# Expert attention with queries on partitions, masked scores in SBUF and 32x64 PE tiles, in a two-stage attention kernel

## The chip, the cores and the metric

One core of a Trainium2 chip runs the whole program. The metric is the time of one execution on the device, in microseconds (us), as the median over runs; for the kernel before it is 646.24 us. "PE" is TensorE's matmul stream, "PEld" its weight loads, DVE is VectorE, ACT is ScalarE, POOL is GpSimd, SP is the SyncE queue that issues nearly all DMAs.

## What is computed

Two attentions in sequence. The first has 4 batches, 8 heads, 768 positions and 64 dimensions; a query only sees keys that fall into its own one of 16 clusters. Its output is `x`, 4 x 768 x 512. The second has 4 experts with causal attention over `x`, each with its own projections, and a gate that keeps two experts a position:

```python
# stage 1, for each batch and head
q_assign = argmax(q_n @ c_n.T); k_assign = argmax(k_n @ c_n.T)
scores = where(q_assign[:, None] == k_assign[None, :], q @ k.T / 8, -1e9)
x_head = softmax(scores) @ v
# stage 2, for each expert e of 4
q, k, v = x @ wq[e], x @ wk[e], x @ wv[e]        # 512 -> 64
scores = where(causal, -1e9, q @ k.T / 8)
ye = softmax(scores) @ v @ wo[e]                  # 64 -> 512
out += (weight of e at this position, 0 if it isn't among the top two) * ye
```

The factors of wq and wk make the second stage's scores large, so its softmax subtracts the true row maximum, and both stages split an operand into a rounded high part and a remainder (`hi`, `lo`) and multiply three products (hi by lo, hi by hi, lo by hi).

## The kernel before

The work is cut into 24 pairs of heads: pairs 0 to 15 are the first stage (four a batch), pairs 16 to 23 the second (two pairs of experts a batch, `ep` 0 and 1). Each step is written as an operation of a `Plan`: its engine, what it needs, which buffers it uses. The order in which operations are issued, over all engines, is a list of numbers written out by hand (`ORDER`; a star picks the other engine that an operation may run on), and a second list (`SLOTS`) says which slot of its tag each buffer gets. Each engine runs its own instructions in that order; PSUM is four slots of two banks (tag `pp`).

Both kinds of pair go through `core(n)` (L829). It has two passes over the scores.

- **The row pass** puts queries on partitions to find each query's maximum: matmuls at L873 (first stage) and L877 (experts: 16 matmuls a pair, of the high parts alone, of 128 to 512 key columns, as the causal triangle needs), for experts the diagonal block's mask added in PSUM (L886), a DVE maximum over the keys (L888), a reduction (L898) and a 32x32-block transpose (L921, L923), and a DMA that writes the maxima as row 48 of the mask half of the tile `tk`.
- **The second pass** puts keys on partitions: for each block of 128 keys the three products and a fourth, `km` by `qm`, that subtracts the maximum and, in the first stage, applies the cluster mask (L960: 8 matmuls a block, of 384, 256 or 128 query columns). ACT takes the exponential from PSUM into a `p` tile (L966), POOL clears the upper triangle of a diagonal block (L971), POOL or DVE adds the `p` tiles of a half up in `acc` (L326, L327: the two engines of one helper), and PE multiplies `p` with the values in fp32 (L1004; `p,vt` in the first stage, `p,vm` for experts), the two heads side by side in two column tiles of 64. An expert pair has nine such blocks: three of the first half (384, 256, 128 columns), six of the second (four of 384, then 256 and 128).

The row sums come from four matmuls of `acc` with ones (L1044, `total`), which stand at the head of the next pair's value product. They go to SBUF (L1048), to DRAM (`sd`) and back as `r`, are inverted (L1067, for experts times the gate `g`), go to DRAM again (`rd`) and come back broadcast over partitions as `rb`; the product with the value result is `xt` in the first stage (L1095), which is stored as `x`. The very last expert pair takes a form of its own without DRAM (`last_half`, L790 to L812). `moe_operands` makes the projections (L666) and `moe_values` the experts' values and gates (L706); `moe_out` multiplies with `wo` (L1133).

Each of the three sets of operands `tk`, `tq` serves every third pair. There are nine `p` tiles, used in turn; one holds 2 x 384 columns.

Of the kernel before, what the change touches and what calls it, by code (L numbers as in the profile page):

```python
# [10 lines left out]
def _warn_once_fixed(msg, *args, **kwargs):  # L11
# [19 lines left out]
MO = dict(pair=25.0, k=-49.5, q=-56.0, v=-45.5, v_step=1.7, x=-43.5, row=-36.5, row_step=2.2, top=30.5, av=17.5,  # L31
          add=40.5, sums=-11.5, norm=52.0, out=26.0, out_step=5.5, keep=10.0, slack=0.05, m_copy=0.1, m_rest=2,
          m_add=4, m_moe=0, m_xt=1, enter=4.0)

ORDER = """
0 19 ~34 1 4 2 31 ~7 5 8 7 56 6 11* 9 3 10 32 12 ~17 20 13* 16* 33 21 55 22 54 35 34 ~13 60 14 147 39 18* 23 61 17* 24
62* 15* ~21 25 148 29 28* 41* 27 30* ~8 70 74 71 68 36 75 80 38 242 72 69 37 78 73 57 79 59 76 58 87 77 63 93 335 85
40 81 94 82 42* 88 83 44 84 86 64 91 241 105 92 100 106 45 114 101 46 108 115 102 109 47 95 103 111 96 104 89 112 117
90 97 66* 98 150 99 243 107 430 48 49 118 121 51 52* 110 53 244 162 50 133 122 163 336 158 134 113 119 159 160 120 127
161 156 116 128 166 43 157 130 167 124 131 123 164 125 136 165 146 168 169 65* 338 170 137 138 561 126 188 145 139 152  # L40
129 177 186 189 140 178 171 187 191 132 172 141 175 200 192 176 142 173 201 135 197 174 179 198 181 144 180 194 190
143 182 195 203 183 154* 184 149 185 151 193 655 196 222 204 213 258 223 537 254 259 219 205 199 255 260 547 220 216
261 560 252 153* 217 214 253 250 215 256 251 225 218 257 228 226 548 275 229 262 231 276 221 245 263 246 232 264 233
224 67 206 234 227 337 294 240 155 271 235 295 202 282 272 236 269 265 283 237 285 230 266 429 280 286 270 288 281
247* 273 289 291 274 267 292 239 207 284 297 268 238 277 278 248* 279 431 432 748 287 308 307 290 298* 367 309 354 368
536 310 538 355 350 311 293 319 208 351 299 352 320 313 353 312 348 314 209 346 349 316 347 344 317 315 322 345 323
325 356 357 318 326 358 327 211 535 300 328 321 550 329 374 334* 296 330 361 388 375 331 362 359 551 389 210 376 360
654 363 324 377 379 364 365 380 369 366 382 340 370 385 332 339 342* 333 301 383 562 386 391 371 372 378 563 373 302
341 437 381 402 401 392* 444 403 384 413 303 445 438 414 416 439 842 541 440 387 417 404 441 448 405 446 449 410 390
447 442 411 407 443 406 408 419 450 451 420 452 305 421 409 393 422 412 423 470 249 428* 461 656 471 482 304 462 459  # L50
483 468 415 394 460 424 479 306 469 425 463 473 480 549 418 464 457 474 453 458 476 434 472 454 455 427 477 485 426
456 475 465 466 395 467 436* 936 478 498 486 495* 579 499 577 580 496 396 481 749 578 594 497 507 595 543 573 508 484
501 574 539 575 502 569 576 397 510 500 570 571 511 504 487 572 433 503 505 513 581 582 514 552 583 515 540* 506 488
516 399 517 599 343 522* 509 518 590 607 600 591 584 608 542* 604 585 519 398 586 605 489 601 587 512 588 602 592 589
613 565 521 593 610 603 490 520 611 596 597 614 616 598 567 545 751 606 564 843 657 435 609 638 617 212 626 673 491
639 665 544* 674 629 612 666 669 1031 630 627 670 671 628 632 672 554 663 631 633 667 664 641 668 635 642 492 684 636
675 644 634 658 645 659 676 646 615 677 493 647 637 685 701 648 698 702 653* 640 680 699 693 681 649 678 695 694 679
650 643 688 618 696 686 689 707 566* 687 682 651 704 619 683 652 705 697 690 845 708 710 691 750 692 660* 620 568 700
721 711 720 759 722 621 661* 723 760 937 761 724 729 762 763 725 730 726 764 757 727 767 1030 758 703 735 768 765 736
732 766 728 752 769 770 753 771 706 733 738 739 740 494 731 712 741 742 709 801 747 743 772 787 802 744 773 734 782  # L60
622 788 774 789 775 795 745 790 737 783 746 792 796 713 776 793 778 755* 777 798 779 780 799 804 781 791 784 785 939
786 623 938 624 714 794 625 815 715 805 814 859 754* 816 817 860 855 818 820 716 856 797 861 821 851 862 829 806 556
558 400 852 853 819 830 826 854 823 827 800 857 824 832 858 863 822 864 833 865 834 803 662 835 825 883 841* 836 874
884 889 875 717 837 872 866 890 828 873 838 881 756 867 892 882 886 893 831 868 887 870 869 839 895 847 885 807 871
876 896 840 898 877 888 878 879 808 844 880 1033 718 809 1032 546* 891 1563 923 908 810 899 947 924 964 948 911 849*
846 965 951 912 909 952 894 945 910 920 946 26 955 921 949 956 913 917 950 953 918 914 954 557* 941 897 915 926 927
957 958 928 959 916 1125 919* 929 989 935 922 962 990 975 930 900 963 966 811 976 980 967 931 812 968 977 981 969 932
925 960 901 978 970 961 986 1564 971 983 848* 933 934 902 984 972 973 987 992 974 1565 940 979 1124 943* 1005 993 1002
# [3 lines left out]
1028 1062 1056 524 1063 1075 1086 905 1027 1035 1057 942* 1066 1067 1068 1076* 906 1037* 1087 1154 1139 1096 1155 1088  # L72
1102 526 1140 1133 1079 1103 1097 1132 1134 1135 1098 1099 1136 559* 1143 1100 1082 1111 1144 998 1141 1112 1158 1142
1108 523 1101 1159 1137 1109 1105 1138 1085 1106 1114 1145 1146 1115 1147 1104 1116 1117 1107 1118 1174 1123 944 1127
553* 1177 1175 1000 1168 1178 1110* 1156 1119 1163 1169 1157 1113 1120 1171 1164 1150 1148 1172 1151 1165 1036* 1129
1121 1149 1152 1122 1166 1180 1153 999 1160 1161 1167 1126 1162 1219 555* 1170* 1190 1229 1173 1181 1233 1230 1193
1234 1566 1235 1194 1191 1089 1131* 1236 1218 1227 1192 1196 1228 1237 1195 1197 1231 1202 1232 1199 1203 1238 1176
1205 1567 1239 1240 1200 1241 1198 1128 1206 1208 1221 1209 1223 1090 1179 1210 1091 529 1182 1201 1211 1092 1259 1217
# [189 lines left out]
def kernel(  # L268
# [66 lines left out]
    def tmp(tag, shape, dt=FT, bufs=1):  # L335
        return plan.buf(sb, tag, shape, dt, bufs)
# [79 lines left out]
    def is_moe(n):  # L416
        return n >= NA
# [420 lines left out]
    def core(n):  # L838
# [199 lines left out]
        if n == NS - 1:  # L1038
            return
# [170 lines left out]
```

## Time and profile before

| | us |
|---|---|
| median of the runs (2: 646.12 and 646.36) | 646.24 |
| span of the profiled execution, first to last instruction | 644.0 |
| PE busy | 634.8 |
| DVE busy | 484.6 |
| POOL busy | 466.9 |
| ACT busy | 302.5 |

How to read it: the profiled execution is one run; its span runs from the first instruction to the last, so the median holds about 2.2 us more than the span. Matmuls are pipelined, and a group's busy time is the union of its instructions from start to end; the distance from one start to the next is what an instruction costs PE. Each PE row shows the array shape used (64*128 is a tile of 64 rows and 128 columns).

### The profile page before, as it was taken

The page shows a single profiled execution, that of the slowest core. Times are in us where ns is not written, and L with a number is a line of the kernel's source. Part 1 is how long each engine was busy: PE and PEld are TensorE (multiplying, and loading weights), DVE is VectorE, ACT ScalarE, POOL GpSimd, SP SyncE. Part 2 cuts the span into 40 slices and gives each one's busy share as a digit, 9 for nine tenths or more (in the row PEclk, how much of TensorE's full clock was granted, in tenths as well). Part 3 has the DMA queues.
Part 4 walks back from the last instruction along what each step waited for, and adds up shares of the span by engine and source line. Part 5 has one row for each costly group of instructions (what it writes and reads, how often), then busy time and mean ns, then how long its engine had stood idle before and what let it go on. Part 6 is the DMA issues. An engine that isn't in the chain of part 4 may idle for free.

```text
span 644.0 us, 13775 instructions
## 1 busy us (share of the span) xinstructions
PE 634.8 (99%) x5404; PEld 482.6 (75%) x5404; DVE 484.6 (75%) x813; ACT 302.5 (47%) x499; POOL 466.9 (72%) x337
## 2 busy tenths in 40 slices
PE   8999999999999999999999999999999999999997
PEld 7667677676776666767757787879879879878775
DVE  5987888798787786888989656574885696678843
ACT  4756546466464654646556323342342423244523
POOL 4399999999999999999999937763754476122500
PEclk9999999999999999999999999999999999999989
DMA  9654445445253323425542310311321220021223
GB/s 192 106 93 95 112 97 113 102 101 106 56 121 99 93 60 86 128 70 107 119 125 75 102 57 2 99 52 51 100 75 28 75 78 24 21 83 68 85 93 131
DMA packets 128119, 55.99 MB, mean 87 GB/s; under 512 B 109820, under 2 KB 117688, under 8 KB 128056
## 3 DMA queue, kind: packets, MB, share of 16 engines
q1 hardware_dynamic: 126488, 54.74, 33.8%
q8 instruction: 42, 0.69, 0.5%
q10 hardware_dynamic: 1568, 0.39, 0.3%
q14 instruction: 21, 0.17, 0.1%
HBM read 39.29 MB, written 15.67 MB: 85 GB/s over the span
## 4 chain that ended last, share of the span: by engine, by line
PE 79%; POOL 14%; issue 2%; DVE 2%; ACT 1%; DMA 0%; SPq 0%; POOLq 0%; ACTq 0%; DVEq 0%
PE pp L960 22%; PE pp L1004 20%; PE pp L666 11%; POOL acc L326 10%; PE pp L873 7%; PE pp L1133 6%; PE pp L706 5%; PE pp L1044 2%; PE pp L877 2%; POOL xt L1095 2%; DVE mx L888 1%; PE pp L522 1%; POOL tk L326 1%; PE pp L1148 1%; POOL tq L326 1%
## 5 line engine op out<-in xcount | busy, mean ns | idle before, releaser
L326 POOL TENSOR_TENSOR acc<-acc,p 128x768 f32<-128x768 f32 (+2 forms) x143 | 249.2, 1752 | 42.0 <-DVE acc L327 38.0
L888 DVE TENSOR_REDUCE mx<-pp 128x2 f32<-128x768 f32 (+1 forms) x224 | 204.2, 943 | 47.8 <-PE pp L873 37.1
L966 ACT ACTIVATE p<-pp 128x768 f32<-128x768 f32 (+2 forms) x264 | 196.8, 773 | 78.4 <-PE pp L960 71.6
L960 PE MATMUL pp<-tq,tk 64*128 64x384 f32 (+2 forms) x1584 | 180.1, 333 | 0.8 <-ACT p L966 0.6
L960 PEld LDWEIGHTS pp<-tq,tk 64*128 64x128 f32 x1584 | 135.7, 186 | 20.7 <-issue 11.9
L1004 PE MATMUL pp<-p,vt 128*64 128x384 f32 x768 | 130.9, 491 | 0.0
L1004 PEld LDWEIGHTS pp<-p,vt 128*64 128x64 f32 x768 | 52.4, 137 | 75.9 <-issue 69.0
L326 POOL TENSOR_TENSOR acc<-p,p 128x768 f32<-128x768 f32 (+1 forms) x41 | 74.3, 1813 | 19.8 <-ACT p L966 18.0
L960 PE MATMUL pp<-tk 49*128 49x384 f32 (+2 forms) x528 | 88.3, 329 | 0.0
L873 PE MATMUL pp<-tk,tq 64*128 64x384 f32 x384 | 69.9, 360 | 1.0 <-ACT ssb L1048 0.7
L873 PE MATMUL pp<-tk 48*128 48x384 f32 x384 | 65.7, 338 | 0.0
L971 POOL TENSOR_SCALAR_AFFINE_SELECT p<-p 128x256 f32<-128x256 f32 x48 | 20.5, 443 | 54.6 <-ACT p L966 53.9
L873 PEld LDWEIGHTS pp<-tk,tq 64*128 64x128 f32 x384 | 48.4, 248 | 6.8 <-issue 2.1
L960 PEld LDWEIGHTS pp<-tk 49*128 49x128 f32 x528 | 50.3, 185 | 0.0
L873 PEld LDWEIGHTS pp<-tk 48*128 48x128 f32 x384 | 49.1, 252 | 0.1
L321 ACT ACTIVATE avu<-pp 128x384 f32<-128x384 f32 x32 | 15.7, 490 | 70.9 <-PE pp L1004 57.1
L886 DVE TENSOR_TENSOR pp<-pp,tri 128x256 f32<-128x256 f32 x48 | 20.6, 428 | 26.5 <-PE pp L877 23.1
L1004 PE MATMUL pp<-p,vm 128*64 128x384 f32 (+2 forms) x288 | 39.6, 420 | 0.0
L1095 POOL TENSOR_TENSOR xt<-avu,rb 128x384 f32<-128x384 f32 x24 | 29.7, 1277 | 11.0 <-DMA rb<-rd 11.0
L1004 PEld LDWEIGHTS pp<-p,vm 128*64 128x64 f32 x288 | 19.3, 137 | 22.6 <-issue 17.9
L327 DVE TENSOR_TENSOR acc<-acc,p 128x768 f32<-128x768 f32 (+2 forms) x23 | 24.7, 1072 | 7.5 <-POOL acc L326 7.5
L706 PE MATMUL pp<-wvh,xh 128*128 128x260 f32 x96 | 27.5, 287 | 0.0
(212 smaller groups left out, 993.5 us busy)
## 6 DMA issues: line engine op xcount, KB each, us to landing
rb<-rd SPq DMA_DIRECT2D x46, 192.0 KB
x<-xt SPq DMA_DIRECT2D x16, 384.0 KB
out_dram<-xt SPq DMA_DIRECT2D x21, 256.0 KB
vt<-in_v_dram SPq DMA_DIRECT2D x52, 96.0 KB
vt<-x SPq DMA_DIRECT2D x12, 384.0 KB
kt<-in_k_dram SPq DMA_DIRECT2D x28, 96.0 KB
qt<-in_q_dram SPq DMA_DIRECT2D x28, 96.0 KB
rw<-rows SPq DMA_DIRECT2D x14, 192.0 KB
```

The costliest lines, as they stand in the source:

```text
L326: ways = [("pool", t_pool(n), lambda: POOL.tensor_tensor(dst(), a(), b(), op=fn)), ("dve", t_dve(n), lambda: DVE.tensor_tensor(dst(), a(), ...
L327: ("dve", t_dve(n), lambda: DVE.tensor_tensor(dst(), a(), b(), op=fn))]
L666: PE.matmul(m()[:, hf, :HW], w_[:, dc, es], x_[dc]()[:, c], start=(i == 0), stop=(i == 3 * DC - 1))
L706: PE.matmul(m()[:, c % 2, :NV], x_[dc]()[:, ts], w_[:, dc, :], start=(i == 0), stop=(i == 3 * DC - 1))
L873: PE.matmul(ps()[:, h, :HW], at, kt[rs, i * HW:(i + 1) * HW], start=(j == 0), stop=(j == 1))
L886: DVE.tensor_tensor(e, e, tri[:, None, :].to_broadcast([128, 2, 128]), op=OP.add)
L888: DVE.tensor_reduce(to, ps()[:, :, :w], axis=AX.X, op=OP.max)
L960: PE.matmul(to, kt[rs, kc * 128:(kc + 1) * 128], by, start=(i == 0), stop=(i == 3))
L966: ACT.activation(pt()[:, :, o_:HW], p()[:, :, o_:HW], AF.Exp, scale=SC)
L1004: PE.matmul(av()[h * 64:(h + 1) * 64, 0, o_:HW], d["vv"](h, kc), pt()[:, h, o_:HW], start=(kc == 0), stop=(kc == nk - 1), tile_position=(0 ...
L1095: e.tensor_tensor(xt().rearrange("d (j u f c) -> d f c u j", j=32, u=4, f=2)[:, par], avu()[:, c].rearrange("d (c u j) -> d c u j", c=HC, ...
L1133: PE.matmul(m()[:, c % 2], a_()[:, ts], w_()[:, ep, :], start=(ep == 0 and i == 0), stop=(ep == EP - 1 and i == 2))
```

## The change

The first stage keeps its computation and, but for small swaps, its old order of operations. What changes are its buffers: the mask half of `tk` becomes a tile of its own (`tz`, list `TM`), and `acc`, `avu` and `rb` become rows of one strip of seven rows.

The experts no longer use `core`. `moe_core` makes one pass with queries on partitions. For each block `cc` of 128 queries (`w` = 128 to 768 keys) PE makes all three products for both heads; DVE adds the causal mask, writes the negated scores to a `p` tile in SBUF and keeps each query's minimum, in one TENSOR_TENSOR_REDUCE a head; ACT takes the exponential in place with that minimum as its bias and sums the row; the sum is inverted and multiplied with the gate on [128, 2] tiles; ACT or DVE scales the row; DVE transposes it by 32x32 blocks into the strip. PE then multiplies with the values in tiles of 32 rows and 64 columns: for each 32 keys, eight fp32 matmuls, one for each group of 32 partitions (32 queries of each block) and head, of 32 to 192 columns. That needs the values repeated in the four partition groups: `vm` is stored to DRAM once a batch (`vd`) and loaded with eight DMAs a pair (`v4`), three quarters of them into the `tz` tiles, which the first stage no longer needs.

The experts' row pass, `km`/`qm` product, maxima's DMAs, diagonal clearing, sums, their DRAM round trips, `last_half` and the gates' DRAM round trip go. The projections, values and output products keep their matmuls, two halves to an operation.

Waits that come with it: a transposed block of pair n may overwrite the strip when the value product of pair n-1 has read it; pair 16's must wait for every `xt` of the first stage, since `acc`, `avu` and `rb` lie in the strip; an operation of pair n's value product needs all twelve transposes (pair 23 is cut in two parts); nine `p` tiles are exactly what one pair fills.

`ORDER` and `SLOTS` are new. Expert operations begin at number 1570. Between pair 15's sums on PE (1560) and the first value product of pair 16 (1692) the new order has on PE: the scores of pair 16 but for its two widest blocks, both projections of pair 18, the values of batch 1, and three score blocks of pair 17. On DVE it has there, after the first stage's last `xt`, the twelve transposes of pair 16 and three reductions of pair 17. Over the whole list 30 of the 96 scalings are given to DVE.

```diff
+    strip = consts.tile([128, NC + 1, S], FT)
     def tmp(tag, shape, dt=FT, bufs=1):
-        return plan.buf(sb, tag, shape, dt, bufs)
+        b = plan.buf(sb, tag, shape, dt, bufs)
+        row = {"acc0": 0, "acc1": 1, "acc2": 2, "avu": 3, "rb": 6}.get(tag)
...
-        TK.append(sb.tile([128, 2, 2 * S], FR, name=f"tk{s}", bufs=1))
-        TQ.append(sb.tile([128, 1, 2 * S], FR, name=f"tq{s}", bufs=1))
+        TK.append(sb.tile([128, 2 * S], FR, name=f"tk{s}", bufs=1))
+        TQ.append(sb.tile([128, 2 * S], FR, name=f"tq{s}", bufs=1))
+        TM.append(sb.tile([128, 2 * S], FR, name=f"tz{s}", bufs=1))
...
+            def go(t=t, c0=c0, size=size):
+                for a in range(4):
+                    dma(t()[32 * a:32 * a + 32],
+                        vd[0].rearrange("(c j) n -> j c n", j=32)[:, c0:c0 + size, 2 * ep * D:2 * (ep + 1) * D])
+            ld = op("sp", issues(4 * [(0.36, 0.9, 3.5)]), go, t0 - 10 + 2 * piece, ready, use)
...
+        if n == NA - 1:
+            m = banks()
+            finish(op("pe", t_av(HW) + 0.1, lambda: total(m), t0 + AT["pair"] + AT["sums"], d["sums"][1], [m] + d["sums"][2], mode=32), m)
+    def moe_core(n):
...
+        for cc in range(NC):
+            w = 128 * (cc + 1)
+            nb = 1 if w <= 512 else 2
+            ps = [banks() for h in range(nb)]
+            pt = [p_tile(n)]
+            pt += pt if 2 * w <= S else [p_tile(n)]
...
+                    for j, (kt, qt) in enumerate(((kh, ql), (kh, qh), (kl, qh))):
+                        for h in range(2):
+                            PE.matmul(to, qt[rs, cc * 128:(cc + 1) * 128], kt[rs, i * w // nb:(i + 1) * w // nb],
+                                      start=(j == 0), stop=(j == 2))
...
+                    DVE.tensor_tensor_reduce(lined(of, h), at(h), tri[:, S - w:] if w <= 512 else
+                                             tri[:, S - w:].rearrange("p (i j) -> p i j", i=2), -1.0, BIG,
+                                             OP.add, OP.min, low()[:, cc, h, None])
...
+                    ACT.activation(of(h), of(h), AF.Exp, bias=low()[:, cc, h, None], scale=-1.0, accum_out=total()[:, cc, h, None])
...
+            o_r = op("dve", 0.11, lambda cc=cc: DVE.reciprocal(r()[:, cc], total()[:, cc]), due + 3.2, [o_r], [small])
...
+                    ACT.activation(of(h), of(h), AF.Copy, scale=r()[:, cc, h, None])
...
+                    if h == 0:
+                        DVE.transpose(to, of(h).rearrange("p (g q) -> p g q", q=128))
+                    else:
+                        DVE.transpose(turned[:, S * (cc + 1):S * (cc + 1) + w], of(h))
...
+                for c in cs:
+                    g = max(c // 4, c0)
+                    for a in range(4):
+                        rs = slice(32 * a, 32 * a + 32)
+                        for h in range(2):
...
+                                PE.matmul(av[a // 2]()[h * D:(h + 1) * D, a % 2, (g - c0) * 32:(c1 - c0) * 32],
+                                          d["v4"][c]()[rs, h * D:(h + 1) * D], by, start=(c == 0), stop=(c == 4 * c1 - 1),
+                                          tile_position=(32 * a, h * D))
...
+                    DVE.tensor_tensor(to(lo)(), src(), to(hi)(), op=OP.subtract)
```

## Rows read from the trace of the kernel before

**Rows 1.** The page's first lines: span, busy time, share and count of PE.

```profile
span 644.0 us, 13775 instructions
PE 634.8 (99%) x5404; PEld 482.6 (75%) x5404; DVE 484.6 (75%) x813; ACT 302.5 (47%) x499; POOL 466.9 (72%) x337
```

**Rows 2.** The stretch after the last first-stage value product: length, each engine, clock, DMA.

```profile
412.00:644.00 232.00, 228.13 (x1798) 188.68 (x1796) 157.30 (x324) 83.81 (x177) 100.91 (x106) 0.99 0.22 70
```

**Rows 3.** The same for L960, L877, L666, L706, each alone: PE and PEld.

```profile
412.00:644.00 232.00, 48.52 (x576) 43.28 (x576) 0.99 0.22 70
...
412.00:644.00 232.00, 16.89 (x114) 9.84 (x112) 0.99 0.22 70
...
412.00:644.00 232.00, 57.90 (x312) 54.13 (x312) 0.99 0.22 70
...
412.00:644.00 232.00, 30.64 (x240) 30.28 (x240) 0.99 0.22 70
```

**Rows 4.** The page's groups: count, busy us, mean ns, idle before.

```profile
L1004 PE MATMUL pp<-p,vm 128*64 128x384 f32 (+2 forms) x288 | 39.6, 420 | 0.0
```

**Rows 5.** Timeline of PE about 421 us: start, length, line, form, count.

```profile
420.21 0.41 PE L877 MATMUL pp<-tk,tq 64*128 64x512 f32 x2
420.44 0.71 PE L960 MATMUL pp<-tq,tk 64*128 64x384 f32 x6
...
421.17 0.53 PE L960 MATMUL pp<-tq,tk 64*128 64x256 f32 x6
...
421.64 0.70 PE L960 MATMUL pp<-tq,tk 64*128 64x384 f32 x6
...
423.12 0.45 PE L960 MATMUL pp<-tq,tk 64*128 64x128 f32 x6
...
423.52 0.50 PE L960 MATMUL pp<-tq,tk 64*128 64x128 f32 x6
```

**Rows 6.** Timeline of PE at 309, 322 and 569 us: fp32 products in column tiles.

```profile
309.57 0.85 PE L1044 MATMUL pp<-acc,ones 128*32 128x384 f32 x8
...
322.73 0.52 PE L522 MATMUL pp<-xk,cbd 128*32 128x384 f32 x2
322.74 0.52 PE L522 MATMUL pp<-xq,cbd 128*32 128x384 f32 x2
...
569.42 4.75 PE L1004 MATMUL pp<-p,vm 128*64 128x384 f32 x36
```

**Rows 7.** Timeline of PE at 621 us: fp32 matmuls of one column, 128 weight columns each.

```profile
620.71 0.35 PE L790 MATMUL pp<-ones,acc 128*128 128x1 f32 x2
620.92 0.36 PE L792 MATMUL pp<-ones,p 128*128 128x1 f32 x2
```

**Rows 8.** Timeline of DVE at 200 us: three reductions without a gap.

```profile
200.10 2.69 DVE L888 TENSOR_REDUCE mx<-pp 128x2 f32<-128x768 f32 x3
```

**Rows 9.** Source view of L384, the one DVE operation with an accumulator: ns, first and last start.

```profile
L384 DVE SCALAR_TENSOR_TENSOR avu<-xh x1: 224/224/224, 2.5 to 2.5; 128x64 f32<-128x64 f32 x1
L384 DVE DVE_READ_ACCUMULATOR avu<-xh x1: 81/81/81, 2.7 to 2.7; 128x1 f32 x1
```

**Rows 10.** Groups by shape: a DVE transpose, a small DVE operation, an ACT one with pointers.

```profile
L568 ACT ACTIVATE rows<-ot,row_bias,row_scale 128x384 fp32r<-128x384 bf16 x14 | 9.8, 702 | 8.3 <-DVE ot L529 8.3
...
L483 DVE STREAM_TRANSPOSE xk<-kt 128x768 f32<-128x768 f32 x7 | 6.6, 945 | 0.6 <-DMA kt<-in_k_dram 0.6
...
L1067 DVE RECIPROCAL r<-r 128x12 f32<-128x12 f32 x23 | 4.8, 210 | 8.2 <-DMA r<-sd 8.2
```

**Rows 11.** Timelines of SP and POOL, 403 to 410 us: a sums' round trip.

```profile
403.66 0.50 SPq L311 DMA_DIRECT2D sd<-ssb  x1
...
404.81 1.15 SPq L311 DMA_DIRECT2D rb<-rd  x2
406.00 0.58 SPq L311 DMA_DIRECT2D r<-sd  x1
...
409.43 1.13 POOL L1095 TENSOR_TENSOR xt<-avu,rb 128x384 f32<-128x384 f32 x1 [4.07 <-DMA rb<-rd]
```

More of the change, by code (lines that the diff above doesn't have):

```diff
@@ L697, in moe_values @@
         NV = E * D + E
-        for c in range(NC):
-            m = banks() if c % 2 == 0 else m
+        for c in range(0, NC, 2):
+            m = banks()
             def go(m=m, c=c):
-                ts = slice(c * 128, (c + 1) * 128)
                 i = 0
@@ L853, in core @@
         for hf in range(2):
-            two = range(HC) if not moe else range(1, HC) if hf else ()
-            maxes, mx = [], tmp("mx", (128, 2, HC, 2), bufs=2) if two else None
+            maxes, mx = [], tmp("mx", (128, 2, HC, 2), bufs=2)
             last = [prev["m_pe"][hf]] if n else []
             for cc in range(HC):
-                w = 128 * (hf * HC + cc + 1) if moe else S
-                nb = 1 if w <= 512 else 2
-                w //= nb
-                for i in range(nb):
+                for i in range(2):
@@ new lines, in core, with go @@
+                    maxes.append(op("dve", t_dve(S), go, due + 0.5, [o], used))
+            wide_mx = tmp("tm", (128, HC, 2, 32), bufs=2) if n + hf == 0 else None
+            if wide_mx:
+                last = [op("pool", 0.4, lambda z=wide_mx: POOL.memset(z().rearrange("p c h j -> p (c h j)"), 0.0), t_r - 20, use=[wide_mx])]
+            def go(hf=hf, mx=mx, wide_mx=wide_mx):
+                to = wide_mx().rearrange("p c h j -> p h c j")[:, :, :, 0] if wide_mx else M32[:, hf, :, :, 0]
+                DVE.tensor_reduce(to, mx(), axis=AX.X, op=OP.max)
@@ L900, in core @@
+            maxes.append(op("dve", 0.13, go, due + 0.6, maxes + last, [mx] + ([wide_mx] if wide_mx else [])))
             due = t_r + DUE["top"] + 6 * DUE["row_step"] * hf
@@ L936, in core @@
         sums = []
[L937 removed]
+        ssb = tmp("ssb", (128, HW), bufs=2)
         halves = []
@@ L940, in core @@
         for hf in range(2):
-            nk = (hf + 1) * HC if moe else NC
             pts, all_exps, acc, acc_ops, av_prev, waiting = [], [], None, [], None, []
-            for kc in range(nk):
-                o_ = max(kc - hf * HC, 0) * 128 if moe else 0
-                w = HW - o_
-                diag = moe and kc >= hf * HC
+            for kc in range(NC):
                 due = t0 + dt * t_in
@@ new lines, in core, with visit @@
+            one = t_av(HW)
+            lead = [P[n - 1]["sums"]] if n and hf == 0 else [P[n + 2]["m1"]] if n + 2 < NA and hf else []
+            pre = one * len(lead) + (0.09 if lead else 0)
+            def visit(go=go, lead=lead, av=av):
+                for x in lead:
+                    x[0](av)
+                go()
+            av_prev = op("pe", pre + NC * one, visit, due + DUE["av"],
+                         [(e, pre + i * one) for i, x in enumerate(waiting) for e in all_exps[i]] +
+                         d["v_ready"] + [y for x in lead for y in x[1]], [av] + d["v_use"], mode=32 if lead else 64)
@@ L1032, in core @@
+            av_prev.leaves = 64
+            for i, x in enumerate(lead):
+                rest = NC * one + one * (len(lead) - 1 - i) + 0.09
+                plan.needs(av_prev, (), x[2], rest)
+                x[3]((av_prev, rest), av)
+            for i, x in enumerate(waiting):
+                plan.needs(av_prev, (), [x[1]], (NC - 1 - i) * one)
             if hf == 0:
@@ L1115, in moe_out @@
         wh, wl = W["wo"]
-        for c in range(NC):
+        for c in range(0, NC, 2):
             final = n == NS - 1
-            late = final and c >= HC
-            m = banks() if c % 2 == 0 else m
-            ot = tmp("rb", (128, DM)) if final and c == NC - 1 else tmp("vt" if late else "xt", (128, DM), bufs=2)
-            due = base(n) + 40 + c if final else t1 + MO["out_step"] * c
+            late = final and c + 1 >= HC
+            m = banks()
+            due = base(n) + 22 + c if final else t1 + MO["out_step"] * c
             o = None
```

729 lines of the change are left out of this document (348 added, 381 removed), and 6 rows, old and new, of the table ORDER.

## The prediction

> **What bounds the kernel now.** I read the page's first lines, then the busy time by stretch, then the PE lines of the expert stage each alone, and last the timelines for the price of single instructions. PE is busy for 634.8 of 644.0 us [rows 1]. After 412 us, where only expert work is left, it is busy for 228.1 of 232.0 us at clock 0.99, while DVE has 157.3 us of work, POOL 100.9 and ACT 83.8 [rows 2]. So the expert stage costs what PE is given to do, and nothing else is near. The first stage keeps its work and order, so I leave its time as it is and look for what PE loses and gains in the experts' 232 us, and whether another engine then takes PE's place.
>
> **What PE loses.** From one start to the next, a product of both heads (two 64-row tiles abreast) costs 0.23 us at 512 columns (420.21 to 420.44), 0.18 at 384 (420.44 to 421.17, four products), 0.12 at 256 (421.17 to 421.64) and 0.10 at 128 (423.12 to 423.52) [rows 5]. The old second pass of a pair is five blocks of 384, two of 256, two of 128, at 0.73, 0.47 and 0.40: 5.4 us. The old row pass is one product of 128, 256, 384, 512, twice 320 (0.15 each, between its neighbours) and twice 384: 1.3 us. Nine value blocks take 4.75 us and the sums 0.85 [rows 6]. As a stream that is 12.3 us a pair, 98 for eight. The busy rows say more: 48.5 for L960, 16.9 for the 114 of L877's 128 instructions that lie in this stretch, so 19.0 for all [rows 3], 39.6 for the values [rows 4], 0.85 for each of seven sums: 113 us. The 15 us between are the heads and ends of bursts (first weights loaded in the open, last product draining): 0.10 us for each of 19 bursts a pair.
>
> **What PE gains.** Scores: three products for each block, 0.30, 0.35, 0.55, 0.69, 0.90 (six of 320) and 1.10 (six of 384): 3.9 us a pair. Values: fp32 takes two passes, and the old stream paid 4.75 us for 36 instructions, two abreast, of 5376 column steps in all [rows 6], 0.88 ns a step. If all eight tiles run abreast, a pass over 32 keys costs 0.17, 0.14, 0.11 and 0.085 us at 192, 160, 128 and 96 columns. At 64 and 32 the weights bound it: a load of 128 columns allows a start each 0.105 us (620.71 to 620.92 for two) [rows 7], so I estimate 0.055 for 64. Four groups of 32 keys, two passes: 8 x 0.62 = 5.0 us. With nine bursts at 0.10 a pair is 9.8 us, eight 78. PE is relieved of 113 - 78 = 35 us. Ends: 27, if bursts cost nothing (98 - 71), and 42, if the new ones have no heads. 644 - 35 = 609.
>
> The value tiles are the least certain price. Four column tiles do run abreast (eight instructions, 0.85 us, where one after another they would take 8 x 0.32) and four of them start within about 0.02 us (322.73, 322.74) [rows 6]; two row tiles run abreast in every product of rows 5. No row has four row tiles, or eight tiles in a steady stream. I take them as abreast, as both kinds are alone. The Trainium skill (TensorE: Matmul & The Clock Gate, section "Wait — 56ns, not 53.3ns?") says that matmul starts never come closer than about 25 ns, however few columns; 384 instructions a pair would then take 9.6 us instead of 5.0, and the sum would be 37 us higher. By the two rows at 322.7 us the trace disagrees for four tiles; for a steady stream no row here tells.
>
> **DVE.** A masked reduction of w columns I price as a PSUM operation of the same width plus an accumulator read. Three reductions of 768 take 2.69 us end to end [rows 8]; at the 0.945 that a transpose of 768 takes [rows 10], one starts 0.87 after the other; the one operation with an accumulator took 0.22 for 64 columns, and the accumulator's read 0.08 [rows 9]. Between 64 and 768 columns that is 1.04 ns a column and 0.16 at the head. Twelve of them (5376 columns): 5.6 + 1.9 + 1.0 = 8.5 us. Twelve transposes, 0.945 for 768 [rows 10], so 0.145 at the head: 5.6 + 1.7 = 7.3. Six reciprocals and some eight gate steps at 0.21 [rows 10]: 3.0. Remainders of projections and values: 3.0. Scalings given to DVE, 30 over eight pairs, about 0.62 each: 2.3. Other starred copies: about 1.5. Sum 25.6 a pair; consecutive ones overlap by 0.075, some 45 of them, so 22.2, say 175 us in all, in a stage of about 232 - 35 = 197. DVE goes from 68% to 89% there. Its bounds are 205 (nothing overlaps) and 165 (small ones hidden).
>
> ACT: 24 operations a pair of 448 columns on average; 384 with two pointers take 0.70 [rows 10], so by proportion at most 0.82 each: 20 us, less DVE's share some 17, and copies of 5: about 22, under PE's. POOL loses nearly everything. The eight value loads a pair cost SP about 4 us of issue at the 0.5 of its rows [rows 11]; a pair lasts some 25 us and they may start when the value product two pairs earlier is through, so I cost them at nothing; without that cover, PE would wait up to 8 us a pair, and outputs and loads of x queue behind them on SP.
>
> **What comes back.** (a) The start. Pair 16's transposes wait for the first stage's last xt: sums 0.85, eviction about 0.7, store to load 2.3 (403.66 to 406.00), two more hops of that kind, 0.2, broadcast 4.6 (404.81 to 409.43), two products of 1.13 [rows 11]: 15.7 us; then twelve transposes and three reductions of pair 17, 8.8: 24.5 us. PE has meanwhile four score blocks (1.9), two projections (48 matmuls at 57.9/312 = 0.186: 8.9), a batch of values (72 at 30.6/240 = 0.128: 9.2) [rows 3], three blocks of pair 17 (2.6) and heads, 24 us. The cover is just enough; I charge 2 us, from 0 to 8. (b) The coupling. The nine p tiles hold one pair, so scores of pair n+1 can't leave PSUM before transposes of n, and those wait for the values of n-1: PE and DVE take turns at 89% and nearly 100%. I charge one wide DVE operation and a burst's head a pair, 1.2, so 10 us; from 0 (as now) to 25. (c) The end. Pair 23 passes scores, reduction, exponential, scaling, transposes and values in line, with only outputs beside them: 5 us more than the present end, 2 to 9.
>
> Sum: 644 - 35 + 2 + 10 + 5 = 626 for the profiled execution. The median lies 646.24 - 644.0 = 2.2 above the span: **628 us**.
>
> **The rivals.** *All of it is gained*: the ends are hidden and the coupling costs nothing, 609 + 2 + 2 = 613. For it, PE is never idle now with DVE at 68%; against it, 89% in a strict order. *DVE becomes the bound*: it is busy from about 417 us on with 205, waits 3 for the last xt, and leaves 13 for the last values, outputs and store: 638, with the median's 2.2 about 641, no change by this measure. It decides when DVE's pair costs over 25 us. *The first values come late*: the sums' chain is as relaxed as round trips are now, 15 us more: 643. *The eight tiles don't run abreast* (the other side, slower): with starts 25 ns apart, or only two row groups at a time, the pair's values cost about 9.8 instead of 5.0: 38 us back, less coupling since PE has more: 609 + 38 + 13 + 2 = 662. Against it stand the four abreast; for it, that nothing shows eight. It decides at 23 ns a start (9 us a pair).
>
> **How the numbers follow.** 2%, some 13 us, is about what a measurement of this kernel can tell from no change, so faster means under 633.3 and slower over 659.2. Chances: the forecast 0.50 (own range 618 to 638), all gained 0.12, DVE 0.22, late values 0.06, tiles 0.10. Faster: 0.12, four fifths of the forecast, a little of DVE's low end: 0.54. Slower: the tiles and the worst of DVE: 0.12. Same: 0.34. For 8 in 10 the range leaves out the tiles, the best part of the full gain and the worst of DVE: 612 to 648.
>
> **What would show it.** Right: PE's score line at about 31 us over eight pairs and the value line at about 40; eight value starts within 0.06 us; DVE near 89% after 417 us; PE's first idle stretch at pair 16's values under 8 us. Wrong: value starts 25 ns apart; reductions of 768 over 1.1 us each; PE idle behind transposes in every pair; PE's clock falling between; SP holding value loads until PE waits for them.

## The result

The changed kernel takes 654.27 us as the median of two runs (652.68 and 655.87) against 646.24 before. The ratio is 1.0114, with a 95% interval of 1.0077 to 1.0151. The forecast was 628, with a range of 612 to 648. So PE was not relieved as foreseen, and the kernel became about 1% slower, which is less than the 2% that the prediction set as the least clear change.

The page of the kernel after: span and PE's line, then the queue that brings the instructions.

```profile
span 650.9 us, 19151 instructions
PE 624.8 (96%) x7944; PEld 483.8 (74%) x7944; DVE 511.0 (79%) x1019; ACT 358.3 (55%) x648; POOL 379.9 (58%) x288
...
q8 instruction: 62, 1.02, 0.7%
```

The same queue on the page of the kernel before:

```profile
q8 instruction: 42, 0.69, 0.5%
```

PE's busy time falls by 10 us [rows 1], but the span grows by 6.9. PE now has 7944 matmuls where it had 5404, and the instruction queue brings 62 packets (of 16 KB, by the trace) where it brought 42. How fast these packets come explains the longest waits below, as the experiments show; it does not explain the whole miss, whose larger part is work that PE still has to do.

The expert stage of the kernel after (after 412 us): all engines, then L1103 (the value product) alone, then L1030 (the scores) alone. Columns as in [rows 2, 3].

```profile
412.00:651.00 239.00, 217.44 (x4342) 186.52 (x4338) 175.35 (x521) 138.56 (x328) 32.34 (x69) 0.98 0.43 108
...
412.00:651.00 239.00, 54.68 (x3264) 48.32 (x3264) 0.98 0.43 108
...
412.00:651.00 239.00, 41.16 (x384) 31.22 (x384) 0.98 0.43 108
```

PE is busy for 217.4 of 239 us, where it was 228.1 of 232 [rows 2]: about 22 us in which it does nothing, the last 5 of them behind its last product. The value line has 54.7 us, not about 40, and the score line 41.2, not 31. DVE has 175.4 us of work, as forecast, but that is 73% of the stage.

What PE waited for in the expert stage of the kernel after (engine, line, releaser: us in total, times, longest):

```profile
PE pp L1103 <- issue: 12.1, 10, 2.1
PE pp L1103 <- DVE strip L1071: 1.2, 1, 1.2
PE pp L1030 <- DVE tq L683: 0.9, 1, 0.9
```

Nearly all of the waiting stands before L1103, and "issue" means that the profile shows nothing that PE waited for. The transposes (L1071) appear once, with 1.2 us, before pair 23's first values. One of the ten "issue" waits is theirs too: the 1.24 us before pair 16's first values (444.97 to 446.21), where the last transpose of that pair ends at 446.13.

The timeline of PE around the longest such wait, kernel after, and the DMA issues of SP just before it:

```profile
475.19 0.91 PE L1103 MATMUL pp<-strip,vm 32*64 32x64 f32 x65
478.17 0.85 PE L1103 MATMUL pp<-strip,vm 32*64 32x32 f32 x63 [2.06 <-issue]
...
471.07 4.80 SPq L308 DMA_DIRECT2D tz<-vd  x8
```

PE stops in the middle of one burst of 128 matmuls. In the trace, the instruction at which it goes on carries no semaphore wait, so it did not wait for data or for another engine. Counting PE's instructions (weight loads, matmuls and the sequencer's semaphores, in order of start) gives the reason. Each of the other nine "issue" waits stands inside a value burst and at the same place of a block of 256:

```
wait (us)             length   index of the next instruction   index modulo 256
454.12 -> 455.38       1.26       8385                            193
476.11 -> 478.16       2.06       9409                            193
534.05 -> 535.65       1.61      11457                            193
572.41 -> 573.06       0.65      12481                            193
599.61 -> 600.26       0.66      13761                            193
613.98 -> 614.43       0.45      14273                            193
624.16 -> 626.08       1.92      15041                            193
632.78 -> 633.20       0.43      15553                            193
637.31 -> 639.09       1.78      15809                            193
```

The busy view by stretches, cut at three of these waits, shows the same count (kernel after; the bracket behind PE is its matmuls, the next one its weight loads):

```profile
614.43:626.08 11.65, 8.49 (x384) 6.96 (x383) 9.29 (x22) 4.62 (x10) 0.40 (x2) 1.00 0.20 72
626.08:633.21 7.12, 6.70 (x256) 5.39 (x255) 3.12 (x11) 1.60 (x5) 0.41 (x2) 1.00 0.02 5
633.21:639.09 5.88, 3.68 (x127) 2.62 (x127) 2.32 (x6) 1.43 (x3) 0.00 (x0) 1.00 0.20 72
```

127 matmuls, 127 weight loads and two semaphore instructions are 256; the two stretches above are two and three times that, to within an instruction at a cut. The nine waits sum to 10.8 us. At none of the nine places is there a semaphore wait, while every other wait of PE over 0.15 us after 412 us ends at an instruction that has one. Each of the nine ends 1.2 to 1.6 us after a 16 KB packet of the instruction queue has come in. That packet began 0.9 to 2.1 us after PE passed the place 256 instructions before, and 3.1 and 3.6 us after it at the waits of 476 and 637 us; why it began late there is open. In the kernel before no wait over 0.15 us stands at such a place.

So the first reading is theory A: *PE waits for its own instructions.* The rivals are theory B, the loads of the repeated values come late, and theory C, the coupling with DVE that the prediction charged with 10 us.

### The profile page after: what moved, and what is told of

The parts are those of the page before. It is cut to its first block, busy times and chain, and to the rows that moved or that the text cites. A ratio compares the mean times of both kernels' runs of the same rounds, so it can differ in the third digit from the quotient of the medians.

```text
span 650.9 us, 19151 instructions
## 1 busy us (share of the span) xinstructions
PE 624.8 (96%) x7944; PEld 483.8 (74%) x7944; DVE 511.0 (79%) x1019; ACT 358.3 (55%) x648; POOL 379.9 (58%) x288
## 4 chain that ended last, share of the span: by engine, by line
PE 81%; DVE 6%; ACT 3%; issue 3%; POOL 3%; DMA 1%; SPq 0%; ACTq 0%; DVEq 0%; POOLq 0%
PE pp L884 20%; PE pp L908 17%; PE pp L819 10%; PE pp L665 9%; PE pp L1103 7%; PE pp L727 5%; PE pp L1154 5%; PE pp L1030 4%; POOL strip L323 3%; PE pp L939 2%; ACT p L1046 2%; PE pp L527 1%; DVE p L1040 1%; DVE strip L1071 1%; DVE strip L1073 1%
## 5 line engine op out<-in xcount | busy, mean ns | idle before, releaser
L323 POOL TENSOR_TENSOR strip<-strip,p 128x768 f32<-128x768 f32 x111 | 206.3, 1867 | 23.5 <-DVE strip L324 13.9
L825 DVE TENSOR_REDUCE mx<-pp 128x2 f32<-128x768 f32 x192 | 176.0, 953 | 41.5 <-PE pp L819 36.9
L888 ACT ACTIVATE p<-pp 128x768 f32<-128x768 f32 x192 | 151.7, 813 | 56.4 <-PE pp L884 50.5
L884 PE MATMUL pp<-tq,tk 64*128 64x384 f32 x1152 | 137.0, 341 | 0.8 <-ACT p L888 0.6
L1046 ACT ACTIVATE p<-p,st 128x640 f32<-128x640 f32 (+5 forms) x96 | 63.3, 661 | 39.1 <-DVE st L1040 34.1
L884 PE MATMUL pp<-tz 49*128 49x384 f32 x384 | 66.5, 336 | 0.4 <-DMA tz<-tm 0.4
L819 PE MATMUL pp<-tz 48*128 48x384 f32 x384 | 66.2, 338 | 0.0
L1040 DVE CUSTOM_DVE_ANT_0 p<-pp,tri 128x640 f32<-128x640 f32 (+5 forms) x96 | 56.1, 612 | 10.7 <-PE pp L1030 10.5
L323 POOL TENSOR_TENSOR strip<-p,p 128x768 f32<-128x768 f32 x28 | 52.2, 1864 | 8.8 <-ACT p L888 8.8
L1103 PE MATMUL pp<-strip,tz 32*64 32x96 f32 (+5 forms) x2496 | 44.1, 273 | 9.1 <-issue 7.3
L1103 PEld LDWEIGHTS pp<-strip,tz 32*64 32x64 f32 x2496 | 38.5, 131 | 16.1 <-issue 13.1
L819 PEld LDWEIGHTS pp<-tz 48*128 48x128 f32 x384 | 49.6, 251 | 0.1
L1030 PE MATMUL pp<-tk,tq 64*128 64x384 f32 (+4 forms) x384 | 41.2, 343 | 1.3 <-DVE tq L683 0.9
L318 ACT ACTIVATE strip<-pp 128x384 f32<-128x384 f32 x22 | 10.8, 490 | 52.4 <-PE pp L908 48.1
```

The source lines that it names most:

```text
L323: ways = [("pool", t_pool(n), lambda: POOL.tensor_tensor(dst(), a(), b(), op=fn)), ("dve", t_dve(n), lambda: DVE.tensor_tensor(dst(), a(), ...
L819: PE.matmul(ps()[:, h, :HW], at, kt[rs, i * HW:(i + 1) * HW], start=(j == 0), stop=(j == 1))
L825: DVE.tensor_reduce(mx()[:, :, cc, i], ps()[:, :, :HW], axis=AX.X, op=OP.max)
L884: PE.matmul(p()[:, h, :HW], kt[rs, kc * 128:(kc + 1) * 128], qt[rs, hf * HW:(hf + 1) * HW], start=(i == 0), stop=(i == 3))
L888: exps = [op("act", t_act(S), lambda p=p, pt=pt: ACT.activation(pt(), p()[:, :, :HW], AF.Exp, scale=SC), due + 0.5, [s_], [p, pt])]
L1030: PE.matmul(to, qt[rs, cc * 128:(cc + 1) * 128], kt[rs, i * w // nb:(i + 1) * w // nb], start=(j == 0), stop=(j == 2))
```

## The experiments

Times are compared through the ratio to the kernel before, measured on the same chip (647 to 649 us there). The sum of waits "at 193" is that of all PE gaps over 0.15 us within two instructions of index 193 modulo 256; the changed kernel has 10.8 us in 9 places. "Half clock" is the time that the trace shows with PE at 1.2 GHz before its last instruction: 3.4 us before, 10.2 in the changed kernel. PE's work is counted from start to start: each matmul is charged the distance to the next one's start, less the time in which neither a matmul nor a weight load ran. By this count the kernel before has 635.0 us of work and 4.1 of idle time, the changed one 625.0 and 19.8.

### Without the value loads

```diff
-                for a in range(4):
-                    dma(t()[32 * a:32 * a + 32],
+                k = size if b == 0 or (ep, c0) == (1, 2 * NC) else 1
+                for a in range(4):
+                    dma(t()[32 * a:32 * a + 32, :k],
```

> From batch 1 on, the loads of the repeated values (tz<-vd) bring one 32-key chunk of twelve; only the quarter that goes to a vm buffer is loaded in full. The tz tiles keep values of batch 0. Theory A (instruction supply): in the changed kernel PE stops for 10.8 us at nine places of the value product, each time at the same place of a 256-instruction block (instruction 193 modulo 256, 1.2 to 1.6 us after a 16 KB instruction block has come in), because 256 of its instructions are used up faster than the next block comes. Without the loads the nine places remain, only the two longest (2.06 us at 476, 1.61 us at 534, both while eight such loads ran) shrink to about 0.5: 647 to 652 us by the median. Theory B (late values): PE waits there for the loads; the waits go, 640 to 643. Theory C (DVE coupling, the one of the prediction): nothing changes, 651 to 655.

Measured: ratio 1.0011 (0.9991 to 1.0031), about 6.7 us under the changed kernel; median 648.29. PE's longest group of waits in the expert stage:

```profile
PE pp L1104 <- issue: 9.1, 9, 2.2
```

The busy view of the same stage:

```profile
412.00:644.00 232.00, 213.68 (x4338) 184.12 (x4334) 173.15 (x521) 138.25 (x327) 32.79 (x69) 0.99 0.29 83
```

The waits stay, 9.1 us, all at 193. So theory B falls, as the missing semaphore waits said already: they aren't waits for values. The time is in A's range, but not quite for A's reason: the waits fell by only 1.7 us. Work fell by 3.3, because the half clock fell to 3.4 us, the same as in the kernel before. That makes this run a useful scale: at the clock of before, the new kernel's PE work is 621.7 us, 13.3 less than the old one's.

### The same program 64 instructions further on

```diff
-    begun = op("pe", t_mm(128), spin, -1e3, use=[front])
+    begun = op("pe", t_mm(128), lambda: [spin() for i in range(33)], -1e3, use=[front])
```

> 32 more matmuls (64 PE instructions) of constants at the very start of the program, nothing else. Theory A (instruction supply): every long wait inside the value product again stands at instruction 193 modulo 256 of PE's whole sequence, so 64 instructions earlier in the product than now (32 matmuls); their sum stays near 11 us (7 to 15), the time within 4 us of the changed kernel plus up to 2 us for the matmuls: 650 to 660. Theories B (late values) and C (DVE coupling): the waits stand at the same matmuls of the value product as now, and the time is 654 to 657.

Measured: ratio 1.0232 (1.0198 to 1.0266), 663.47 us. All eleven long waits inside value and score bursts stand at 193 again, now 64 instructions earlier in the program, and sum to 16.2 us. Two rows of the timeline show one that now falls into a score burst:

```profile
544.20 0.98 PE L1030 MATMUL pp<-tk,tq 64*128 64x384 f32 x7
549.26 0.89 PE L1030 MATMUL pp<-tk,tq 64*128 64x384 f32 x5 [4.09 <-issue]
```

A score block of twelve matmuls is broken after its seventh for 4.09 us; in the changed kernel no score block is broken. Nothing but the count of instructions differs, so the place of the waits belongs to the instruction sequence and to no tile. This is the cleanest evidence for A. The time was above what A gave: waits 5.4 us longer, 20.5 us at half clock.

### Half of the value tiles

```diff
-                        for a in range(4):
+                        for a in range(4 if c in (0, 4 * c1 - 1) else 2):
```

> Of the value product's eight tiles only the four of partition groups 0 and 1 are computed, but for the first and the last 32 keys of a product (the other queries' results are left wrong). PE's value work falls by about 22 of 53 us and its instructions by about 2,800. Theory A (instruction supply): blocks of 256 instructions last longer, the 10.8 us of waits go to under 2, and the half-clock spells that follow them too: 654 - 22 - 10 - 3 = 619, 614 to 625. Theory B (late values): the loads are as late as before, 632 or more. Theory C (DVE coupling): PE is relieved but DVE (175 of 239 us) is not, 635 to 645.

Measured: ratio 0.9817 (0.9796 to 0.9838), 635.56 us. The busy view of the value product alone:

```profile
412.00:636.00 224.00, 46.29 (x1776) 41.24 (x1776) 0.97 0.46 114
```

PE's waits in the expert stage:

```profile
PE pp L665 <- DVE st L1040: 1.7, 1, 1.7
PE pp L1103 <- DVE strip L1071: 1.4, 1, 1.4
...
PE pp L1154 <- issue: 0.4, 1, 0.4
```

The waits on "issue" are gone (10.8 to 0.4 at 193), with the same loads and the same DVE work. That is A's mark. But the time fell by 19 us, not by 35, because my price for the work was wrong. With nearly half of the matmuls left out, the value product's work (start to start) fell only from 53.2 to 44.9 us. Four tiles cost nearly what eight cost, so the eight do run abreast. By its time alone this run falls into the ranges of B and C; the waits decide it.

### Short transposes

```diff
-                        DVE.transpose(turned[:, S * (cc + 1):S * (cc + 1) + w], of(h))
+                        k = w if n == NA else 32
+                        DVE.transpose(turned[:, S * (cc + 1):S * (cc + 1) + k], of(h)[:, :k])
```

(the other head's likewise)

> From pair 17 on each of the twelve transposes of a pair covers 32 columns instead of 128 to 768; the rest of the strip keeps what pair 16 left. DVE loses about 5 us a pair, some 36 us in all. Theory A (instruction supply): DVE was not what PE waits for, 651 to 655. Theory C (DVE coupling, charged with 10 us in the prediction): at least 8 us faster, under 646.

Measured: ratio 1.0072 (1.0041 to 1.0103), 652.17 us. The busy view of the expert stage:

```profile
412.00:653.00 241.00, 219.13 (x4352) 187.35 (x4348) 142.58 (x521) 139.91 (x329) 33.65 (x70) 0.98 0.43 107
```

PE's longest group of waits in it:

```profile
PE pp L1105 <- issue: 13.5, 11, 2.1
```

DVE lost 32.8 of 175.4 us and the kernel about 2.7, with overlapping intervals. Theory C, as what holds up the changed kernel, falls.

### Other work between the bursts

Fifteen of PE's steps change their place in `ORDER`; three of them, with names in the place of the list's numbers:

```diff
-... av23A.0  av23A.1  out3.2a ...
+... av23A.0  out3.2a  av23A.1 ...
-... av19.2  s20.5 ...
+... s20.5  av19.2 ...
-... q23  av21.0 ...
+... av21.0  q23 ...
```

(av: a value burst of a pair, s: a score block, q: a projection, out: an output product)

> Same instructions; 15 of PE's steps change their place in the order of the expert stage, so that other work stands between the bursts of the value product (15 moves of one step past one or two others, with what hangs on it; three PSUM slots differ). Chosen with a small model of PE alone: durations from the trace of the changed kernel, and the next 256 PE instructions are there 3.3 to 4.4 us after the last block of 256 was begun. For the order of the changed kernel this model gives 6 to 24 us of waits, for the new one 0.2 to 7. Theory A (instruction supply): waits at instruction 193 modulo 256 fall from 10.8 to about 2, and the half-clock spells behind them go too: 640 to 646 us. Theory B (late values): the waits come from loads, which are issued as before: 650 to 656. Theory C (DVE coupling): value products that end later hold up transposes, 655 to 662.

Measured: ratio 1.0726 (1.0673 to 1.0780), 694.52 us, far slower. PE's waits in the expert stage:

```profile
PE pp L1095 <- issue: 7.5, 5, 3.7
PE pp L1095 <- DVE strip L1063: 6.4, 3, 4.5
PE pp L1022 <- DVE st L1032: 5.7, 7, 1.7
PE pp L1022 <- DVE tq L675: 3.8, 2, 1.9
PE pp L657 <- DVE st L1032: 3.3, 4, 1.1
```

The waits at 193 did fall, to 5.4 us (the 3.7 us on "issue" stand at the head of pair 16's values, not at 193). But 35.9 us of other waits after 412 us came (5.4 in the changed kernel): projections and scores held back let DVE's reductions and transposes come late, and PE then waits for them. The half clock rose to 54.6 us. A model of PE alone could not see this. The chain through DVE costs little in the order as it is, and much once it is pulled.

### Loads in long runs

The stores to the new layout; the loads read it:

```diff
-            dma(vd[0].rearrange("(c p) n -> p c n", p=128), vm())
+            for a in range(4):
+                for i in range(EP):
+                    dma(vd[0][i].rearrange("j (c a) n -> j c a n", a=4)[:, :, a], vm()[32 * a:32 * a + 32, :, 2 * i * D:2 * (i + 1) * D])
```

> The DRAM copy of the values (vd) is laid out so that each partition of a load reads one run of 6 KB where it read twelve of 512 bytes; eight stores a batch in the place of one. Same bytes. Theory A (instruction supply, stretched where loads run): the loads occupy the DMA engines for a shorter time, the longest waits shrink as they did without the loads: 648 to 652. Theory A without the stretching: waits unchanged, 653 to 656.

Measured: ratio 1.0112 (1.0077 to 1.0146), 655.10 us, the same as the changed kernel; 12.5 us of waits at 193. The length of the runs in DRAM made no difference that these runs show. Whether the loads stretch the waits stays open: without them they shrank by 1.7 us, which is no more than they differ between kernels that don't touch them.

### Narrow value matmuls

```diff
+                                e1 = c1 if c in (0, 4 * c1 - 1) else g + 1
+                                by = by[:, :e1 - g]
-                                ... (g - c0) * 32:(c1 - c0) * 32],
+                                ... (g - c0) * 32:(e1 - c0) * 32],
```

> Every matmul of the value product covers 32 columns instead of 32 to 192, but for the first and the last 32 keys of a product (the result is left wrong). The same number of instructions; PE's value work falls by about 13.8 us (384 starts a pair at the 10.1 ns of the 32-column form). Theory A (instruction supply): the instructions come no faster, so that waits rise by 7 to 9 us and only 5 to 7 are saved: 647 to 650. Theories B (late values) and C (DVE coupling) without any limit on instructions: 640 to 643.

Measured: ratio 1.0198 (1.0148 to 1.0248), 660.36 us: not faster than the changed kernel but rather slower (the intervals just touch), with far less to compute. The expert stage:

```profile
412.00:659.00 247.00, 222.10 (x4351) 189.84 (x4346) 174.44 (x521) 139.97 (x329) 33.94 (x70) 0.89 0.43 105
```

The value work fell by 7.7 us, not 13.8. The waits at 193 rose by 2.6 to 13.4. The granted clock is 0.89 (0.98 in the changed kernel), with 54.6 us at half clock, which makes scores and outputs dearer by 8 us. No theory had this. What is left of A's claim is that less work at the same number of instructions gained nothing, and the clock has a part in that.

### The bursts joined

```diff
-... av16.0  s17.1  s17.0  av16.1  s18.2  s17.3  av16.2 ...
+... av16.0  av16.1  av16.2  s17.1  s17.0  s18.2  s17.3 ...
```

(and so for each pair)

> The two or three bursts of each value product follow each other at once in PE's order; nothing else is moved. 17 changes to the 32x64 tiles and back are saved, with about 0.15 us each, 2 to 3 us. Theory A (instruction supply): 768 instructions in one go last 5.7 us by their work and 10 to 11 by their supply; waits rise by 17 to 20 us: 665 to 675. Theories B (late values) and C (DVE coupling) without any limit on instructions: 648 to 656.

Measured: ratio 1.0925 (1.0879 to 1.0972), 708.05 us. PE's two longest groups of waits in the expert stage:

```profile
PE pp L1094 <- issue: 34.5, 17, 3.7
PE pp L1021 <- DVE st L1031: 5.6, 7, 1.7
```

The busy view of the stage:

```profile
412.00:706.00 294.00, 240.36 (x4344) 206.04 (x4340) 173.37 (x521) 138.67 (x328) 33.15 (x69) 0.85 0.35 88
```

Theories B and C, without a limit on instructions, gave 648 to 656. The waits on "issue" are three times as long, all at 193. The value products of pairs 16 to 20 now last 9.3 to 12.9 us each. Of the 55 us by which PE ends later, 32 are idle time and 23 dearer work: the clock is 0.85, with 85 us at half. A's direction is right; its size was too small. The dearer work goes with the lower clock, and the waits that are not at 193 rose from 5.4 to 13.7 us.

### Two moves and five moves

Two of the fifteen moves, chosen to hold back no score, projection or load: `av23B.1` behind `out3.4a`, `av23A.1` behind `out3.2a`.

> As the changed kernel, with two of the fifteen moves: the second burst of the last pair's first value product comes behind the output product that followed (av of pair 23, one of 1.65 us), and its very last burst behind another output product. No score, projection or load moves. Theory A (instruction supply): of the waits at instruction 193 modulo 256 the last three of the changed kernel (1.92, 0.43 and 1.78 us) fall to under 1.5 together: 2 to 4 us faster, 650 to 653 where the changed kernel has 654 to 655. Without any limit on instructions: 654 to 656.

Measured: ratio 1.0144 (1.0120 to 1.0167), 657.51 us, no gain. The last waits at 193 fell from 4.1 to 2.7 us, less than expected; the others grew (one from 1.26 to 2.63), and the sum stayed at 10.8. As a way to win the waits back it failed.

With `av17.2`, `av19.2` and `av21.2` each behind one score block as well:

> The two moves, and the last value burst of pairs 17, 19 and 21 behind one score block of a later pair. Theory A (instruction supply) and nothing else late: another 1 to 4 us, 647 to 651. If what the fifteen moves showed decides (a step that is held back keeps PSUM slots and transposes from the next ones, and PE then waits for those): 653 to 660.

Measured: ratio 1.0132 (1.0095 to 1.0170), 656.03 us. PE's waits in the expert stage:

```profile
PE pp L1095 <- issue: 4.8, 6, 1.8
PE pp L1022 <- DVE st L1032: 3.6, 5, 1.4
PE pp L1146 <- DVE xq L1115: 2.7, 2, 1.5
...
PE pp L1146 <- issue: 1.2, 1, 1.2
```

The waits at 193 fell from 10.8 to 6.0 us, and the others rose from 5.4 to 10.7: what the instructions no longer take, the chain through DVE does. So the coupling of the prediction exists, but in this order it shows only when the waits for instructions shrink. Moving PE's steps gained nothing in the three orders tried, and no version here that computes the whole result beats the kernel before.

## Why the prediction was wrong

Its sum was 35 us of relief for PE and 17 us that come back. By the two traces the account is: work at equal clock 13.3 less (from the run without loads), the half clock 3.4 more (6.8 us more at half speed), waits for instructions 10.8, other waits 4.9, the end behind PE's last product 1.1 (5.0 in place of 3.9). That is 6.9, by which the span grew.

The step that failed is PE's relief: 13.3 us where 35 were forecast, which with the half clock is about the whole miss of the span (650.9 for 626). It failed mainly in the price of the value product, and less in the reading of the busy rows, both below. The 17 us that come back were met by 16.8 (idle time 15.7, the end 1.1), but by luck: most of them are waits for instructions, a mechanism that the prediction did not have. Without these 10.8 us and the 3.4 of the half clock the span would be about 637; that is an estimate from this account, and no run shows it.

**What PE loses** was too high: 113 us, where the distances from start to start give 107.5. In the expert stage L960 takes 44.1 of them, close to the stream price of 5.4 us a pair, L877 13.9, the values 38.4, the sums and the last pair's form 11.1. The wrong step is the reading of the busy rows [rows 3] as cost to PE: they gave L960 48.5 and L877 19.0. A line's busy time runs to the end of its last matmul, while the next line has already started, so much of the "heads and ends" was counted for two lines. The error is smaller in the sum, by luck: 5.6 us of the last pair's own form and the gates (L753 to L805) were left out of the 113. Without them 101.9 remain, 4 above the stream of 98 and not 15.

**What PE gains** was too low: 78 us is the new work as forecast, where 92.5 were measured, and 90.9 at the clock of before (107.5 - 90.9 = 16.6; the 3.3 us to the 13.3 above lie in other lines, the projections and the first stage's scores above all, which the prediction left as they were). The scores are near (37.9 for 36, at the clock of before). The values are not: 53 for 42, the largest single error. Three rows of the timeline of the kernel after, pair 18, with the start of what follows each burst:

```profile
508.64 2.67 PE L1103 MATMUL pp<-strip,tz 32*64 32x192 f32 x128
511.24 0.96 PE L1030 MATMUL pp<-tk,tq 64*128 64x512 f32 x6
...
513.72 2.06 PE L1103 MATMUL pp<-strip,tz 32*64 32x128 f32 x128
515.71 0.50 PE L1154 MATMUL pp<-s,xk 128*128 128x512 f32 x1
...
518.69 1.54 PE L1103 MATMUL pp<-strip,tz 32*64 32x64 f32 x128
520.16 0.61 PE L665 MATMUL pp<-xh,wkh 128*128 128x384 f32 x2
```

2.60, 1.99 and 1.47 make 6.06 us for an undisturbed pair where 5.3 were forecast. From one start to the next a matmul takes 19.6 ns at 192 columns, 16.2 at 160, 14.9 at 128, 14.1 at 96, 10.7 at 64 and 10.1 at 32. The widest form is as priced (0.157 us for a pass of eight, forecast 0.17); the narrow ones are dearer, 0.113 for 0.085 at 96 columns, 0.086 and 0.081 for 0.055 at 64 and 32. That is 5.5 us of stream for 5.0. The rest is 0.13 to 0.31 for each burst in place of 0.10, the last pair in two parts (2.2 more), and, as far as can be told, bursts that the coming of their instructions slowed without a full stop.

**The eight tiles abreast**, the least certain price, was right: in the burst at 508.64 eight starts lie within 0.047 us (6.7 ns apart; 0.06 was the sign asked for) with over 0.1 us to the next eight, 64 starts of the widest form take 1.25 us, and half of the tiles cost nearly what all cost. The rule that matmul starts never come closer than about 25 ns (the Trainium skill, TensorE: Matmul & The Clock Gate, section "Wait — 56ns, not 53.3ns?") does not hold for these tiles: six forms lie between 10.1 and 19.6 ns. Its result came close for another reason. Joined, 384 matmuls took 9.3 to 12.9 us, which is 24 to 34 ns each, mostly because their instructions came no faster (a part of it at half clock). The kernel is between the forecast and that rival.

**DVE** was right in work (175 us) and wrong in weight: the stage it stands in is 239 us long, not 197.

**What comes back**, term by term: the first values of pair 16 came 1.24 us late, where 2 were charged. The end cost 1.1 behind PE and 1.24 before the last pair's values, under the 5 charged. The coupling, charged with 10, shows about 1.3 (before score blocks 0.41 behind a reduction, L1040, and 0.88 behind a remainder of a projection, L683). The 10.8 are waits for instructions, and the prediction had no step for them. Its own list had the means: 384 value matmuls with as many weight loads, in bursts that it priced at 5 us a pair, are three blocks of 256 instructions. What it lacked was the question how fast a block can come. The row that answers it is on no page of the kernel before as a wait; the instruction queue's line was there, with 42 packets in 644 us, about one in 15 us.

The Trainium skill (Runtime: NRT & Kernel Launch, section Instruction fetch mechanics) says that an engine's instructions are fetched in 16 KiB blocks of 256 by a DMA queue of its sequencer's own, while the block before is executed, and that this is mostly hidden because instructions are dispatched more slowly than they come. The traces agree on block and queue. Here it is not hidden: matmul and weight load of the narrow tiles go out at 5 to 10 ns an instruction, 1.3 to 2.5 us a block, and where PE waited a block took 3.2 us at the least.

**The signs of being wrong** named the clock. It did fall, 0.99 to 0.98 in the stage. In the changed kernel the three spells at 1.2 GHz begin 0.4 to 1.4 us after waits for instructions; but the narrow matmuls brought 54.6 us at half clock with only 2.6 us more of waits. So waits are not the only cause, and what else is stays open.

## What to carry to other kernels

Splitting a product into many small tiles buys array time with instructions: before believing the gain, divide the time of each dense burst by its PE instructions (weight loads count) and compare a block of 256 with the 3.2 to 6.0 us that one took here where PE waited. A stop in the middle of a burst whose operands are already there, on "issue", at equal distances in PE's instruction count, is the sign; extra instructions at the start of the program move it. Count what a line costs PE from start to start, not by its busy time, and look for the next wait behind the one that you remove: in two of the reordered kernels here the other waits grew by as much or more.

## What the runs showed of the hardware

- PE's next 256 instructions come in one 16 KB packet that takes 0.9 to 1.7 us; PE goes on 1.2 to 1.6 us after it. From one such boundary to the next, where PE waited, passed 3.2 to 6.0 us in the changed kernel. Bursts of 256 instructions that took 1.5 to 2.7 us therefore stopped PE unless slower work stood beside them. Longest waits: 2.06 us in the changed kernel, 4.09 in the shifted one.
- 64 instructions at the start of the program cost about 7.6 us (2.4 of them for the matmuls themselves): the boundaries fell into denser stretches, and more time passed at half clock.
- Eight fp32 tiles of 32x64 run abreast, with starts 10.1 to 19.6 ns apart on average; leaving four of them out saved 8.3 of 53.2 us, together with 46% of the matmuls.
- A kernel with less to compute was no faster: with value matmuls of 32 columns the granted clock of the stage was 0.89, where it was 0.98.
